# Pair's outputs stored from seven places, a third's operands made in pieces, next pair's raw loads bound to units

## The chip, the cores and the metric

The kernel runs on one core of a Trainium2 chip. The metric is the device time of one execution in microseconds (us); smaller is better. The engines are named as in the profile: PE (TensorE, matmuls), DVE (VectorE), ACT (ScalarE), POOL (GpSimd), SP (SyncE, which here only issues transfers).

## The reference, cut to what matters

Linear attention, then a gated feed-forward layer with an RMS norm, then a second feed-forward layer, in which the change lies:

```python
def _moe2_ref(x, w1, w2, w3, w_out) -> np.ndarray:
    h = np.maximum(np.maximum(x @ w1, x @ w2), x @ w3)
    return (h @ w_out).astype(np.float32)
# x 4608x512, w1, w2, w3 512x768, w_out 768x512, all float32
```

## The kernel before, in words

The 4608 tokens are nine groups of 512. Attention and the first layer run group by group and leave their results in device memory (`x2_dram`). The second layer then takes the first eight groups two at a time, which the code calls a **pair**, and the ninth alone. For a pair, `x @ w` is a two by two block product computed with seven block products instead of eight (A11, S2, S1, S3, A12, S4, A22 against the operands B11, T2, T1, T3, B21, B22, T4); three of the seven add onto a PSUM bank that already holds another.

Every float32 factor is split into a high and a low part, and each block product is six matmuls of 128x128 by 128x512 (`product2`, L488 to L494 in `three`). A **unit** is one weight matrix for one third of the 768 columns: seven block products, 42 matmuls, in four PSUM banks (G, V, a0, a1). A pair has nine units; three in a row (one for each of w1, w2, w3) make a **third**, and their maximum is kept in four SBUF tiles `t` (tags q, k, v, t; two buffers each). In a unit, PE fills the banks in the order A11 to G, S2 to V, S1 to a0, S3 to a1, then A12 onto G, S4 onto a0, A22 onto a1. Between them the other engines work: ACT copies G to `s1` (L749), DVE adds V to make `u2` (L751), ACT copies a0 to `s5` (L753), POOL adds the two to `w` (L754), and DVE adds `w` and a1 (L743 in the first unit of a third, else L745 followed by the maximum in L746). Only when that addition has read a1 may PE start A22, which adds onto a1.

When a third is done, `h_operands` makes its seven operands for the output product: four DVE subtractions (L797 to L810), and for each operand a high part cast by ACT (L91) and a low part subtracted by DVE (L92), eleven DVE and seven ACT instructions. For the first two thirds this code stands right behind the third's last unit. Behind the ninth unit, `out_pair` multiplies all three thirds with `w_out`, in eight banks, and gives eight output tiles of 128x512: two copied by ACT (L867), six added by DVE (L845). Each tile is written into one of three buffers (tag y) and stored to device memory from there.

Weights come from device memory in chunks of three block products (768 KB) through a ring of six tiles; a chunk is fetched into a ring place as soon as PE has read the old one (`consumed`). `load_raw` fetches the next pair's two groups (four tiles of 256 KB and two of 512 KB), and `combine` makes the four sums T1 to T4 from them with eight DVE subtractions (L603). A scheduler sorts instructions within what the data allow, and may pull code ahead of where it is written; each engine then runs its own list strictly in order, and SP issues all chunk fetches, raw loads and most stores from one list.

Of the kernel before, what the change touches and what calls it, by code (L numbers as in the profile page):

```python
# [15 lines left out]
P = 128  # L16
# [30 lines left out]
def attention_moe_moe(ctx: ExitStack, tc: tile.TileContext, q, k, kt, v, w1, rms_g, w2, w2_out, out):  # L47
# [486 lines left out]
                evacuate(acc[g][m], x2_dram[g][:, m, :], f"xe_{g}", m, 0.5)  # L534


    ring, fetched = {}, [0]
    wanted = [(p, c, None) for p in range(NPAIR) for c in range((UNITS + OUTS) * QUARTERS // CHUNK)]
    turns = [0, 1, 2, 3, UNITS, 4, 5, 6, 7, 8, UNITS + 1, UNITS + 2]
    single = [chunk_of(u, n) for u in turns for n in (A11, A12, S1, A22)]  # L540
# [2 lines left out]
    def fetch(count=1):  # L543
        for _ in range(count):
            i = fetched[0]
            if i >= len(wanted):
                return
            p, c, parts = wanted[i]
            t = wpool.tile([P, CHUNK, 2, N // 2], F32R, tag=RING[i % len(RING)], name=f"chunk_{p}_{c}")
            if parts is None:  # L550
                nc.sync.dma_start(t.bitcast(F32), chunk_dram[c])
            else:
                for n, (c, i) in enumerate(parts):
                    nc.sync.dma_start(t[:, n].bitcast(F32), chunk_dram[c][:, i])
            ring[p, wanted[fetched[0]][1]] = t
            fetched[0] += 1
# [170 lines left out]

    temps = []

    def unit(pr, u, t):  # L730

        fp, j = divmod(u, 3)
        a, b, c, d = (bank(tag, f"p2_{pr}_{u}_{tag}") for tag in ("G", "V", "a0", "a1"))
        if not temps:
            for tag in ("wh9", "wl9"):
                x = place(f"temps_{tag}", tag)
                temps.extend(x[:, i, :] for i in range(3))
        s1, s5, u2, w, y0, y1 = temps
        n = QUARTERS * u

        def largest(dst, x, pt, y):
            if j == 0:
                nc.vector.tensor_add(dst, x, pt)  # L743
            else:
                nc.vector.tensor_add(y, x, pt)  # L745
                nc.vector.tensor_max(dst, dst, y)  # L746

        product2(a, pr, n + A11, B11, True, True)
        nc.scalar.copy(s1, a)  # L749
        product2(b, pr, n + S2, T2, True, True)  # L750
        nc.vector.tensor_add(u2, s1, b)  # L751
        product2(c, pr, n + S1, T1, True, True)
        nc.scalar.copy(s5, c)  # L753
        nc.gpsimd.tensor_add(w, u2, s5)  # L754
        product2(d, pr, n + S3, T3, True, True)
        largest(t[1, 1], w, d, y0)
        product2(a, pr, n + A12, B21, False, True)
        if j == 0:
            nc.scalar.copy(t[0, 0], a)
        else:  # L760
            nc.vector.tensor_max(t[0, 0], t[0, 0], a)
        product2(c, pr, n + S4, B22, False, True)
        largest(t[0, 1], u2, c, y1)
        product2(d, pr, n + A22, T4, False, True)
        largest(t[1, 0], u2, d, y0)
# [58 lines left out]
        r = (2 * row + m) * P  # L824
        queue.dma_start(out[r : r + P, g * N : (g + 1) * N], e)

    def out_place(name):
        return two.tile([P, N], F32, tag="y", name=name, bufs=3)

    def out_pair(pr, t):  # L830
        g = 2 * pr
        a, b, c, d = ([bank(tag, f"o_{pr}_{tag}") for tag in tags] for tags in (
# [4 lines left out]
        for (pts, n, which), later in zip(steps, ((T1, T2), (T3, B21), (B22, T4), ())):  # L837
            out_product(pts, pr, n, which, (0, 1), True, False, False)
            for x in later:
                h_operands(2, t, x)  # L840
        u, w = temps[0:2], temps[2:4]

        def add(x, pt, row, col, m):
            e = out_place(f"oe_{pr}_{row}{col}_{m}")
            nc.vector.tensor_add(e, x, pt)  # L845
            store(e, row, g + col, m, nc.sync)

# [13 lines left out]
        for pts, n, which in ((a, A12, B21), (c, S4, B22), (d, A22, T4)):  # L861
            out_product(pts, pr, n, which, (0, 1, 2), False, True, True)
            consumed(pr, QUARTERS * UNITS + OUTS * (OUT_ORDER.index(n) + 1))
            for m in range(2):
                if n == A12:
                    e = out_place(f"oe_{pr}_00_{m}")
                    nc.scalar.copy(e, a[m])  # L867
                    store(e, 0, g, m, nc.scalar)
                elif n == S4:
                    add(u[m], c[m], 0, 1, m)  # L870
                else:
                    add(u[m], d[m], 1, 0, m)
# [7 lines left out]
            fetch()  # L880

    for pr in range(NPAIR):
        for u in range(UNITS):
            fp, j = divmod(u, 3)
            if j == 0:
                t = {
                    key: two.tile([P, N], F32, tag=tag, name=f"t2_{pr}_{fp}_{tag}")
                    for key, tag in (((0, 0), "q"), ((0, 1), "k"), ((1, 0), "v"), ((1, 1), "t"))
                }
            unit(pr, u, t)  # L890
            consumed(pr, QUARTERS * (u + 1))
            if pr == 0 and u == 0:
                out1(NG - 1, NF1 - 1)
                h_places()
            if j == 2 and fp < 2:
                for which in (B11, T1, T2, T3, B21, B22, T4):
                    h_operands(fp, t, which)
            if u == 1:
                load_raw(pr + 1)
            if 3 <= u < 7:  # L900
                for n in range(2 * u - 6, 2 * u - 4) if pr + 1 < NPAIR else range(2) if u == 3 else ():
                    combine(pr + 1, n)
        out_pair(pr, t)
        for which in range(7) if pr + 1 < NPAIR else (B11, B21, T1):
            split_operand(which)
# [114 lines left out]
```

## Time and profile before

| what | value |
|---|---|
| time, three runs | 1567.25 us median (1562.35, 1567.25, 1567.54) |
| time of the profiled execution | 1566.17 us |
| its span, first to last instruction | 1564.1 us |
| outside the span | 2.07 us |
| matmul busy time | 1519.6 us, 97% of the span |
| DVE, ACT, POOL busy time | 937.4, 568.7 and 217.8 us |
| mean granted TensorE clock | 0.992 of full speed |

The span is the program on the engines; the time adds what lies around it. A matmul's row in a trace is longer (0.39 us) than the step from one start to the next (0.23 us), because matmuls overlap; starts tell the pace. The second layer fills the span from about 1012 us to its end.

### The profile page before, as it was taken

Reading aid. Unit: us, or ns where it says so; the run is one execution under the profiler, and the core shown is the slowest. Engines: PE = TensorE matmul, PEld = TensorE weight load, DVE = VectorE, ACT = ScalarE, POOL = GpSimd, SP = SyncE. Lnnn points to the kernel's source line nnn. Section 1 sums busy time; section 2 is a strip of 40 time slices with the busy share of each in tenths; the row PEclk is TensorE's granted clock in tenths of the full one; section 3 lists DMA queues with packets and bytes.
Section 4 is the critical chain, followed back from the end, with each engine's and each line's share of the span. In section 5 each row is a group of like instructions: output and inputs, shape, how many; then the busy total and the mean of one; then the engine's idle time right before and its main releaser. Section 6 shows DMA issues by size and latency. Waiting matters only on the chain.

```text
span 1564.1 us, 18927 instructions
## 1 busy us (share of the span) xinstructions
PE 1519.6 (97%) x6902; PEld 1251.6 (80%) x6902; DVE 937.4 (60%) x1622; ACT 568.7 (36%) x1079; POOL 217.8 (14%) x279
## 2 busy tenths in 40 slices
PE   6899999999999999999999999999999999999999
PEld 4677888888888888888888888877877877877887
DVE  6999846655656666566553244556856846737622
ACT  6764533434334334334342232232422422413311
POOL 0000321221211221302212000011111101101100
PEclk8899999999999999999999999999999999999999
DMA  7842431432423324404313022155765665665473
GB/s 271 322 145 78 169 103 43 153 107 63 146 91 116 125 67 141 140 26 159 118 40 102 1 95 94 41 200 179 266 216 181 240 231 182 210 234 186 170 264 107
DMA packets 97837, 227.74 MB, mean 146 GB/s; under 512 B 9168, under 2 KB 33744, under 8 KB 97744
## 3 DMA queue, kind: packets, MB, share of 16 engines
q1 hardware_dynamic: 90832, 213.94, 40.9%
q10 hardware_dynamic: 6912, 12.59, 2.2%
q8 instruction: 55, 0.90, 0.2%
q14 instruction: 38, 0.31, 0.1%
HBM read 183.50 MB, written 42.99 MB: 145 GB/s over the span
## 4 chain that ended last, share of the span: by engine, by line
PE 82%; DVE 10%; DMA 3%; ACT 2%; POOL 1%; issue 1%; SPq 0%; DVEq 0%; ACTq 0%; POOLq 0%
PE pg L488 6%; PE pg L486 6%; PE pg L487 6%; PE pv L488 6%; PE pv L486 6%; PE acc L494 6%; PE acc L493 6%; PE pv L487 6%; PE acc L492 6%; PE p_a L492 3%; PE p_a L494 3%; PE p_a L493 3%; DMA out<-oe 2%; PE pk L326 2%; PE p_G L494 2%; PE p_G L493 2%
## 5 line engine op out<-in xcount | busy, mean ns | idle before, releaser
L658 DVE SCALAR_TENSOR_TENSOR t<-t,pg 128x512 f32<-128x512 f32 x106 | 72.7, 686 | 131.9 <-ACT t L657 130.3
L672 ACT CAST hh<-t 128x512 fp32r<-128x512 f32 x108 | 66.9, 620 | 154.0 <-DVE t L669 153.5
L676 DVE TENSOR_TENSOR hl<-t,hh 128x512 fp32r<-128x512 f32 x108 | 80.5, 745 | 54.5 <-ACT hh L672 53.8
L754 POOL TENSOR_TENSOR temps_wl<-temps_wh 128x512 f32<-128x512 f32 x36 | 48.8, 1355 | 457.0 <-ACT temps_wh L753 367.0
L492 PE MATMUL p_a<-x_wh,chunk 128*128 128x512 f32 x240 | 95.3, 397 | 16.1 <-DVE t_t L743 8.1
L657 ACT ACTIVATE t<-pg 128x512 f32<-128x512 f32 x106 | 62.9, 594 | 131.8 <-PE pg L488 131.8
L669 DVE TENSOR_TENSOR t<-t,pv 128x512 f32<-128x512 f32 x108 | 73.6, 682 | 60.6 <-PE pv L488 59.3
L231 POOL TENSOR_TENSOR wq<-st,wq 128x256 fp32r<-128x256 f32 x84 | 63.7, 773 | 221.0 <-ACT wq L230 218.0
L494 PE MATMUL p_a<-x_wh,chunk 128*128 128x512 f32 x240 | 93.9, 391 | 0.0
L493 PE MATMUL p_a<-x_wl,chunk 128*128 128x512 f32 x236 | 92.2, 391 | 0.0
L492 PEld LDWEIGHTS p_a<-x_wh,chunk 128*128 128x128 f32 x240 | 45.3, 189 | 30.6 <-DVE t_t L743 11.5
L749 ACT COPY temps_wh<-p_G 128x512 f32<-128x512 f32 x36 | 21.1, 587 | 118.0 <-PE p_G L494 95.6
L494 PEld LDWEIGHTS p_a<-x_wh,chunk 128*128 128x128 f32 x240 | 45.4, 189 | 9.6
L493 PEld LDWEIGHTS p_a<-x_wl,chunk 128*128 128x128 f32 x236 | 44.5, 188 | 9.2
L751 DVE TENSOR_TENSOR temps_wh<-temps_wh,p_V 128x512 f32<-128x512 f32 x36 | 24.6, 684 | 43.1 <-PE p_V L494 41.5
L290 POOL TENSOR_TENSOR q<-q,qm 128x512 f32<-128x512 f32 x28 | 30.8, 1099 | 125.5 <-DVE qm L281 103.6
L745 DVE TENSOR_TENSOR temps_wl<-temps_wl,p_a 128x512 f32<-128x512 f32 x24 | 16.4, 685 | 52.7 <-POOL temps_wl L754 52.7
L492 PE MATMUL p_G<-x_wh,chunk 128*128 128x512 f32 x123 | 47.9, 389 | 0.0
L494 PE MATMUL p_G<-x_wh,chunk 128*128 128x512 f32 x123 | 47.9, 389 | 0.0
L230 ACT CAST wq<-st 128x256 fp32r<-128x256 f32 x84 | 33.5, 420 | 32.4 <-DMA w_dram<-wq 23.9
L326 PE MATMUL pk<-v,k 128*128 128x129 f32 x300 | 39.8, 280 | 0.3 <-issue 0.3
L302 POOL TENSOR_TENSOR q<-q,qr 128x512 f32<-128x512 f32 x28 | 29.2, 1044 | 75.1 <-DVE qr L301 70.7
(681 smaller groups left out, 4468.9 us busy)
## 6 DMA issues: line engine op xcount, KB each, us to landing
chunk<-w_dram SPq DMA_DIRECT2D x112, 768.0 KB, 4.3
w_dram<-wq SPq DMA_DIRECT2D x84, 256.0 KB, 2.2
words<-in_w SPq DMA_DIRECT2D x24, 768.0 KB, 7.9
chunk<-w_dram SPq DMA_DIRECT2D x48, 256.0 KB, 3.7
k<-in_k SPq DMA_DIRECT2D x30, 320.0 KB, 3.6
v<-in_v SPq DMA_DIRECT2D x30, 320.0 KB, 4.1
st<-in_w SPq DMA_DIRECT2D x18, 512.0 KB, 4.6
x<-xe ACTq DMA_DIRECT2D x36, 256.0 KB, 2.5
```

Of the source, the lines that this page charges most:

```text
L231: nc.gpsimd.tensor_sub(t[:, 1, :], src, t[:, 0, :].bitcast(F32))
L326: nc.tensor.matmul(pk[:, 0 : P + 1], k_t[g, p][:, c, :], v_t[g, p][:, c, :], start=(c == 0), stop=(c == 4))
L486: nc.tensor.matmul(pt, hi[:, j, s], xhs[kk], start=(kk == 0), stop=False)
L487: nc.tensor.matmul(pt, hi[:, j, s], xls[kk], start=False, stop=False)
L488: nc.tensor.matmul(pt, lo[:, j, s], xhs[kk], start=False, stop=(kk == 3))
L492: nc.tensor.matmul(pt, ah, bh, start=first, stop=False, skip_group_check=onto)
L493: nc.tensor.matmul(pt, ah, bl, start=False, stop=False, skip_group_check=onto)
L494: nc.tensor.matmul(pt, al, bh, start=False, stop=last, skip_group_check=onto)
L658: nc.vector.scalar_tensor_tensor(t, t, 1.0, pg, op0=ALU.add, op1=ALU.mult)
L669: nc.vector.tensor_mul(t, t, pv)
L672: nc.scalar.copy(hh[g, f], t)
L676: nc.vector.tensor_sub(hl[g, f], t, hh[g, f].bitcast(F32))
```

## The change

Three things change, all in the second layer. **Stores.** `out_pair` writes its eight outputs into three tiles of tag y, the four tiles `t` of the last third (which nothing reads any more) and once more a tile of tag y, instead of only the three tiles of tag y. **Pieces.** The operands of a finished third are no longer written in one stretch: they are put into four groups (B11 and T1; T2; T3; B21, B22 and T4), and each group is bound behind one of the four DVE steps of the next unit (`u2`, then the three `largest`). `tc.issue_after` binds the scheduler's order and adds no wait by itself. **Raw loads and sums.** The next pair's raw loads are bound behind the chunk fetch last issued at unit 1, and its eight sums behind the DVE steps of units 4 and 5, four each.

```diff
@@ fetch
-                nc.sync.dma_start(t.bitcast(F32), chunk_dram[c])
+                fetches.append(nc.sync.dma_start(t.bitcast(F32), chunk_dram[c]).ins)
@@ unit
+        def then(ins):
+            with tc.issue_after(ins.ins):
+                for step, args in behind.pop(0) if behind else ():
+                    step(*args)
+
         def largest(dst, x, pt, y):
             if j == 0:
-                nc.vector.tensor_add(dst, x, pt)
+                then(nc.vector.tensor_add(dst, x, pt))
             else:
                 nc.vector.tensor_add(y, x, pt)
-                nc.vector.tensor_max(dst, dst, y)
+                then(nc.vector.tensor_max(dst, dst, y))
...
-        nc.vector.tensor_add(u2, s1, b)
+        then(nc.vector.tensor_add(u2, s1, b))
@@ out_pair
+        places = [two.tile([P, N], F32, tag="y", name=f"oe_{pr}_{i}", bufs=3) for i in range(3)]
+        places += [t[key] for key in ((0, 1), (1, 1), (1, 0), (0, 0))]
+        places.append(two.tile([P, N], F32, tag="y", name=f"oe_{pr}_3", bufs=3))
...
-            e = out_place(f"oe_{pr}_{row}{col}_{m}")
+            e = places.pop(0)
@@ the loop over pairs
-            unit(pr, u, t)
+            if 3 < u < 6 or u > 6:
+                todo = (range(0, 4) if u == 4 else range(4, 8) if u == 5 else ()) if pr + 1 < NPAIR else range(2) if u == 5 else ()
+                behind = [[(combine, (pr + 1, n))] for n in todo]
+            unit(pr, u, t, behind)
...
             if j == 2 and fp < 2:
-                for which in (B11, T1, T2, T3, B21, B22, T4):
-                    h_operands(fp, t, which)
+                behind = [
+                    [(h_operands, (fp, t, which)) for which in group]
+                    for group in ((B11, T1), (T2,), (T3,), (B21, B22, T4))
+                ]
             if u == 1:
-                load_raw(pr + 1)
-            if 3 <= u < 7:
-                for n in range(2 * u - 6, 2 * u - 4) if pr + 1 < NPAIR else range(2) if u == 3 else ():
-                    combine(pr + 1, n)
+                with tc.issue_after(fetches[-1]):
+                    load_raw(pr + 1)
```

The order of instructions shows what this moves. DVE, first pair, where its third unit ends and its fourth (`p_0_3`, the first of the second third) begins. Before, with the first third's operands made in one stretch (tiles `h_...`, and `t_0_0_...` for the differences):

```order
L797 TENSOR_TENSOR t_0_0_q<-t_0_0_k,t_0_0_q 128x512
L746 TENSOR_TENSOR t_0_0_v<-t_0_0_v,temps_wl_8550 128x512
L803 TENSOR_TENSOR t_0_0_k<-t_0_0_t,t_0_0_k 128x512
L92 TENSOR_TENSOR h_xl_8634<-t_0_0_q,h_xl_8633 128x512
L92 TENSOR_TENSOR h_ql<-t_0_0_v,h_qh 128x512
L800 TENSOR_TENSOR t_0_0_q<-t_0_0_t,t_0_0_q 128x512
L92 TENSOR_TENSOR h_xl_8636<-t_0_0_k,h_xl_8635 128x512
L751 TENSOR_TENSOR temps_wh_8549<-temps_wh_8549,p_0_3_V 128x512
L92 TENSOR_TENSOR h_xh_8632<-t_0_0_q,h_xh_8631 128x512
L743 TENSOR_TENSOR t_0_1_t<-temps_wl_8550,p_0_3_a_8810 128x512
```

The same place in the change:

```order
L757 TENSOR_TENSOR temps_wh_8549<-temps_wh_8549,p_0_3_V 128x512
L92 TENSOR_TENSOR h_xh_8630<-t_0_0_q,h_xh_8629 128x512
L803 TENSOR_TENSOR t_0_0_q<-t_0_0_k,t_0_0_q 128x512
L92 TENSOR_TENSOR h_xl_8634<-t_0_0_q,h_xl_8633 128x512
L749 TENSOR_TENSOR t_0_1_t<-temps_wl_8550,p_0_3_a_8792 128x512
L806 TENSOR_TENSOR t_0_0_q<-t_0_0_t,t_0_0_q 128x512
L92 TENSOR_TENSOR h_xh_8632<-t_0_0_q,h_xh_8631 128x512
L749 TENSOR_TENSOR t_0_1_k<-temps_wh_8549,p_0_3_a_8791 128x512
L809 TENSOR_TENSOR t_0_0_k<-t_0_0_t,t_0_0_k 128x512
L749 TENSOR_TENSOR t_0_1_v<-temps_wh_8549,p_0_3_a_8792 128x512
```

The unit's `u2` (L751, now L757) has moved ahead of all operand work, and three pieces now stand between it and the addition that reads a1 (L743, now L749). DVE in the next unit (`p_0_4`) of the change; before, nothing stood between these steps:

```order
L92 TENSOR_TENSOR h_kT<-t_0_0_t,h_sacc 128x512
L816 TENSOR_TENSOR t_0_0_q<-t_0_0_v,t_0_0_q 128x512
L757 TENSOR_TENSOR temps_wh_8549<-temps_wh_8549,p_0_4_V 128x512
L603 TENSOR_TENSOR sums_a<-raw_1_4_8718,raw_1_0_8710 128x512
L92 TENSOR_TENSOR x_wl_8538<-t_0_0_q,x_wl_8538 128x512
L751 TENSOR_TENSOR temps_wl_8550<-temps_wl_8550,p_0_4_a_8868 128x512
L752 TENSOR_TENSOR t_0_1_t<-t_0_1_t,temps_wl_8550 128x512
L603 TENSOR_TENSOR sums_a<-raw_1_4_8718,raw_1_1_8712 128x512
L767 TENSOR_TENSOR t_0_1_q<-t_0_1_q,p_0_4_G 128x512
```

Two of the next pair's sums (L603) and the last piece of T4 (`x_wl_8538`) have come in ahead of the maximum that reads G (L767). DVE at the end of the first pair, where `oe` and `o_` are `out_pair`'s tiles and banks and `p_1_0` is the next pair's first unit; before:

```order
L603 TENSOR_TENSOR sums_a<-raw_2_2_9554,sums_b 128x512
L603 TENSOR_TENSOR sums_b<-raw_2_3_9556,sums_b 128x512
L845 TENSOR_TENSOR oe_01_0_9367<-temps_wh_8549,o_acc_9205 128x512
L845 TENSOR_TENSOR oe_01_1_9370<-temps_wh_8549,o_a_9206 128x512
L845 TENSOR_TENSOR oe_10_0_9393<-temps_wh_8549,o_acc_9207 128x512
L751 TENSOR_TENSOR temps_wh_8549<-temps_wh_8549,p_1_0_V 128x512
L845 TENSOR_TENSOR oe_10_1_9396<-temps_wh_8549,o_a_9208 128x512
```

And in the change:

```order
L851 TENSOR_TENSOR oe_0_9275<-temps_wh_8549,o_acc_9207 128x512
L851 TENSOR_TENSOR oe_1_9276<-temps_wl_8550,o_a_9208 128x512
L851 TENSOR_TENSOR t_0_2_t<-temps_wh_8549,o_acc_9205 128x512
L851 TENSOR_TENSOR t_0_2_v<-temps_wh_8549,o_a_9206 128x512
L851 TENSOR_TENSOR t_0_2_q<-temps_wh_8549,o_acc_9207 128x512
L851 TENSOR_TENSOR oe_3_9278<-temps_wh_8549,o_a_9208 128x512
L757 TENSOR_TENSOR temps_wh_8549<-temps_wh_8549,p_1_0_V 128x512
```

The sums have left this place, and three of the last four outputs go to tiles `t_0_2_...` that no store occupies. SP's list keeps its stores where they were; the raw loads of pairs 2 and 3 and of the ninth group move from between chunks 24 and 27 of the pair before to one block behind chunk 9 of the pair in which they are written, and those of pair 1 from behind chunk 5 to behind chunk 9 of pair 0.

## Rows read from the trace of the kernel before

**Rows 1.** The page: busy time, share of the span, instructions.
```profile
PE 1519.6 (97%) x6902; PEld 1251.6 (80%) x6902; DVE 937.4 (60%) x1622; ACT 568.7 (36%) x1079; POOL 217.8 (14%) x279
```

**Rows 2.** Waits of PE: engine and line, waited for, us in total, times, longest.
```profile
PE p_a L492 <- DVE t_t L743: 8.1, 8, 1.0
PE p_a L492 <- DVE oe L845: 8.0, 5, 2.3
```

**Rows 3.** Timeline of PE, pair 0, fourth unit: start, duration, [idle before <-releaser].
```profile
1052.68 0.39 PE L494 MATMUL p_a<-x_wl,chunk 128*128 128x512 f32 x1
1054.08 0.50 PE L492 MATMUL p_a<-x_wh,chunk 128*128 128x512 f32 x1 [1.02 <-DVE t_t L743]
1054.42 0.39 PE L493 MATMUL p_a<-x_wh,chunk 128*128 128x512 f32 x1
```

**Rows 4.** Timeline of DVE and POOL in that unit.
```profile
1050.88 0.68 DVE L751 TENSOR_TENSOR temps_wh<-temps_wh,p_V 128x512 f32<-128x512 f32 x1
1051.47 0.68 DVE L92 TENSOR_TENSOR h_xh<-t_q,h_xh 128x512 fp32r<-128x512 f32 x1
1051.70 1.61 POOL L754 TENSOR_TENSOR temps_wl<-temps_wh 128x512 f32<-128x512 f32 x1 [10.19 <-DVE temps_wh L751]
1053.34 0.69 DVE L743 TENSOR_TENSOR t_t<-temps_wl,p_a 128x512 f32<-128x512 f32 x1 [1.18 <-POOL temps_wl L754]
```

**Rows 5.** Timeline, pair 0: third unit from its first matmul to the fourth unit's.
```profile
1035.23 0.39 PE L492 MATMUL p_G<-x_wh,chunk 128*128 128x512 f32 x1
...
1038.21 0.69 DVE L751 TENSOR_TENSOR temps_wh<-temps_wh,p_V 128x512 f32<-128x512 f32 x1 [1.38 <-PE p_V L494]
...
1039.56 0.59 ACT L753 COPY temps_wh<-p_a 128x512 f32<-128x512 f32 x1 [2.19 <-PE p_a L494]
...
1040.22 1.29 POOL L754 TENSOR_TENSOR temps_wl<-temps_wh 128x512 f32<-128x512 f32 x1 [8.23 <-ACT temps_wh L753]
...
1041.55 0.69 DVE L745 TENSOR_TENSOR temps_wl<-temps_wl,p_a 128x512 f32<-128x512 f32 x1 [2.64 <-POOL temps_wl L754]
1042.27 0.69 DVE L746 TENSOR_TENSOR t_t<-t_t,temps_wl 128x512 f32<-128x512 f32 x1
...
1042.99 0.63 ACT L91 CAST h_sacc<-t_t 128x512 fp32r<-128x512 f32 x1 [2.85 <-DVE t_t L746]
...
1044.75 0.39 PE L492 MATMUL p_G<-x_wh,chunk 128*128 128x512 f32 x1
```

**Rows 6.** Timeline of ACT, DVE and PE at the end of pair 0.
```profile
1123.08 0.59 ACT L867 COPY oe<-o_acc 128x512 f32<-128x512 f32 x1 [2.83 <-PE o_acc L494]
...
1131.39 0.59 ACT L867 COPY oe<-o_G 128x512 f32<-128x512 f32 x1 [7.72 <-DMA out<-oe]
...
1136.84 0.69 DVE L845 TENSOR_TENSOR oe<-temps_wh,o_acc 128x512 f32<-128x512 f32 x1 [9.45 <-DMA out<-oe]
...
1138.18 0.50 PE L492 MATMUL p_a<-x_wh,chunk 128*128 128x512 f32 x1 [2.20 <-DVE oe L845]
...
1140.80 0.50 PE L492 MATMUL p_a<-x_wh,chunk 128*128 128x512 f32 x1 [0.72 <-DVE oe L845]
```

**Rows 7.** Stretches: us, busy time of PE, PEld, DVE, ACT, POOL, PEclk, DMA share, GB/s.
```profile
1378.00:1380.00 2.00, 1.03 (x4) 0.86 (x5) 1.77 (x3) 0.38 (x1) 0.00 (x0) 1.00 0.10 39
1380.00:1384.00 4.00, 4.00 (x12) 3.12 (x11) 1.15 (x3) 0.79 (x2) 1.27 (x1) 0.57 0.94 266
```

**Rows 8.** Timeline of POOL and DVE in pair 0's ninth unit.
```profile
1099.98 1.35 POOL L754 TENSOR_TENSOR temps_wl<-temps_wh 128x512 f32<-128x512 f32 x1 [8.23 <-ACT temps_wh L753]
...
1100.10 1.79 DVE L92 TENSOR_TENSOR x_wl<-sums_a,x_wh 128x512 fp32r<-128x512 f32 x1
```

**Rows 9.** Transfers, 1012 to 1400 us, for chunk and raw: issue to landing.
```profile
DMA to landing us min/median/max: 4.0/4.3/10.1
...
DMA to landing us min/median/max: 2.9/3.8/5.4
```

**Rows 10.** Transfers out of the output tiles, 1012 to 1500 us.
```profile
DMA to landing us min/median/max: 2.0/5.6/7.9
```

More of the change, by code (lines that the diff above doesn't have):

```diff
@@ L534, in out1 @@
                 evacuate(acc[g][m], x2_dram[g][:, m, :], f"xe_{g}", m, 0.5)
-    ring, fetched = {}, [0]
+    ring, fetched, fetches = {}, [0], []
     wanted = [(p, c, None) for p in range(NPAIR) for c in range((UNITS + OUTS) * QUARTERS // CHUNK)]
@@ L728, in attention_moe_moe, with unit @@
     temps = []
-    def unit(pr, u, t):
+    def unit(pr, u, t, behind):
         fp, j = divmod(u, 3)
@@ L825, in store @@
         queue.dma_start(out[r : r + P, g * N : (g + 1) * N], e)
-    def out_place(name):
-        return two.tile([P, N], F32, tag="y", name=name, bufs=3)
     def out_pair(pr, t):
@@ L865, in out_pair @@
                 if n == A12:
-                    e = out_place(f"oe_{pr}_00_{m}")
+                    e = places.pop(0)
                     nc.scalar.copy(e, a[m])
@@ L882, in attention_moe_moe @@
     for pr in range(NPAIR):
+        behind = []
         for u in range(UNITS):
```

## Prediction

> **What bounds the kernel now.** I read the page first. PE is busy 97% of the span [rows 1], so only its waits can be won back. In the list of waits by pair of engines, two entries of PE lie in the second layer [rows 2]: eight waits for the DVE addition that reads bank a1 (t_t L743, 8.1 us) and five for the output additions (oe L845, 8.0 us). The other waits of PE lie in attention's start, far from the change.
>
> Next the timeline at one of each kind. After a wait of 1.02 us the start-to-start step is 1.40 us and the next 0.34 us [rows 3]. The normal step is a unit's 9.52 us over 42 matmuls, 0.227 us [rows 5]. So one such wait costs 1.17 + 0.11 = 1.28 us, 0.27 more than its idle time.
>
> Why PE waits there: in the fourth unit `u2` starts at 1050.88 and `w` runs on POOL at 1051.70, for 1.61 us, so that DVE adds `w` and a1 at 1053.34 [rows 4]. The unit began at 1044.75 [rows 5], so `u2` came 6.13 us into it; in the third unit it came at 1038.21 - 1035.23 = 2.98 us. DVE worked through the finished third's operands first. The eight waits are four pairs times two such thirds.
>
> At the end of pair 0, ACT's second output copy waits 7.72 us for a store of an earlier output and DVE's third addition 9.45 us [rows 6]. Only three places exist, and a store needs 2.0 to 7.9 us to land [rows 10]. Behind those additions PE waits 2.20 and 0.72 us, because the next unit wants banks a0 and a1. Three pairs' ends show it, the last pair's does not: five waits.
>
> At the third of these ends the granted clock was 1.00 over 1378 to 1380 us, in which PE was busy for only 1.03 of 2 us, and 0.57 over 1380 to 1384 us: the lower of its two levels, 1.2 GHz, for the greater part of those 4 us [rows 7]. A share x at half speed gives 1 - x/2 = 0.57, so x = 0.86, 3.4 us; half of it, 1.7 us, was lost.
>
> **What can be won.** Thirds: 8.1 + 8 x 0.27 = 10.3 us. Pair ends: 8.0 + 5 x 0.27 = 9.4 us. Clock: 1.7 us. Together 21.4 us.
>
> **The change part by part.** *Stores.* An output product per half is 9 matmuls, 9 x 0.227 = 2.04 us. The first half of A12 was ready when ACT copied it at 1123.08 [rows 6]; so the halves come ready near 1122.9, 1124.9, 1126.9, 1129.0, 1131.0 and 1133.0 us. The second to fifth go to the four `t` tiles, which nothing occupies. The last takes the first output's place again. That place was free by 1131.4, when ACT wrote its second copy there [rows 6], before 1133.0 us, and the first addition now comes sooner. Even 4 us more would be hidden, since the next unit wants a1 only after three more products, 3 x 1.36 = 4.08 us (a product is 6 matmuls, 1.36 us). The next unit's `s1` and `u2` follow on time. DVE also loses eight sums from this place, which frees it earlier. I take the full 9.4 us and the clock's 1.7 us.
>
> On the fall of the clock the Trainium skill has a rule: the page "TensorE: Matmul & The Clock Gate", section "What's actually happening", says that the low clock is the default, that activity lifts it, and that the window over which the chip judges this runs free of the kernel. The trace agrees in that of three similar pauses one was followed by a fall. By that rule any of the three ends may pay 1.7 us in a given run, so this term would be 0 to 5.1 us; by the rows it is 1.7 us.
>
> *Pieces, in the first unit of the next third.* All times from that unit's start. DVE's back-to-back step is 0.60 us (1050.88 to 1051.47) [rows 4]. `u2` at 2.98; B11's low part 3.6; T1's difference 4.2 to 4.9. ACT's `s5` starts at 4.33 and ends at 4.92 as in the third unit [rows 5]; its cast of T1 (about 0.6 us) ends at 5.6. POOL's `w` runs 4.99 to 6.28 [rows 5]. Here a contention enters: a DVE subtraction of two SBUF tiles that started 0.12 us after such a `w` took 1.79 us instead of 0.68, until 0.56 us after `w` had ended [rows 8]. So T1's low part, which would start at 5.6, ends near 6.9; then a1's addition, 6.9 to 7.6. PE wants it at 6 x 1.36 = 8.16. No wait, with 0.56 us to spare. Between both ends: all eight waits gone, or, if the pieces hold the addition as long as now, none. I take gone.
>
> *The next unit.* T2 to T4 fill DVE: T2's difference 7.5, its low part 8.9 (ACT's copy of G, ready at 5 x 1.36 = 6.8, comes before the cast), a0's addition 9.5, T3's difference 10.1, a1's second addition 10.7, three low parts 11.3 to 13.1, T4's difference 13.1 to 13.8. `u2` then comes at 13.7 instead of 9.52 + 2.98 = 12.5, one sum at 14.3, T4's low part 14.9 to 15.6. ACT casts T4 at 13.8 to 14.4, so `s5` slips from 13.85 to 14.4 to 15.0. `w` meets T4's low part, waits for it and runs 15.6 to 16.8. a1's addition 16.85 to 17.55, due at 9.52 + 8.16 = 17.68. The maximum in t follows 0.72 us after it (1041.55 to 1042.27) [rows 5], 17.6; the second sum 18.2; the maximum that reads G 18.8 to 19.5. PE wants G at 2 x 9.52 = 19.04. A new wait of about 0.45 us, 0.72 us with its restart, in the three pairs that have sums there: 2.2 us. Bounds: 0 without the contention, and 3 x 1.3 = 3.9 us at the length of today's waits. I take 2.2, as the worked one. Behind the second third nothing of sums stands there, so the maximum comes 0.6 us earlier, inside its time.
>
> Units 4 and 5 carry 13 and 12 DVE steps, 7.8 us at most of 9.52; unit 3 has 15, 9.0 us. Total DVE work is unchanged.
>
> *Raw loads.* They stand behind chunk 9, whose ring place is free when PE has read chunk 3, 12 products, 16.3 us into the pair. The first sum wants them at 4 x 9.52 + 3.6 = 41.7 us. Six loads land 2.9 to 5.4 us after issue [rows 9], so even one after another (6 x 5.4 = 32) the last would be only 7 us late, and they overlap. Chunk 10 queues behind them: place free at 15 products, 20.4 us, wanted at 30 products, 40.8 us, against landings of 10.1 us at the slowest. Cost nothing; hidden under units 1 to 3.
>
> The skill's page "DMA: Bandwidth & Descriptors", section "Rules for kernel authors", says to issue a transfer early and wait for it late. This part does the reverse of its first half; by that rule the sums would stall. The trace's 25 us between issue and use speak against a stall here.
>
> **Sum.** 21.4 - 2.2 = 19.2 us gained. The profiled execution took 1566.17 us, so 1547.0; on the median, 1567.25, it would be 1548.0. I say 1547.
>
> **Rivals.** *A, the pieces only move the wait.* DVE runs its list in order, so anything late in the three pieces (ACT's cast of T1, which stands behind `s5`) holds a1's addition, as now. For it: only 0.56 us to spare. Against: ACT has no other work there. It decides if T1's low part ends past 7.5 us. Then the thirds keep 10.3 us: 1566.2 - 21.4 + 10.3 + 2.2 = 1557.
>
> *B, the pair ends stay.* If the last place is not free, or stores queue behind the four chunk fetches of that time, DVE waits as before in front of the next `u2`. It decides when the first output's place is free 5 us later than 1131.4. Keeping 11.1 us: 1566.2 - 10.3 + 2.2 = 1558.
>
> *C, slower: raw loads.* If a raw tile lands later than 25 us after its issue, DVE's list stops at the first sum, and PE a few products later. Each us of it counts three times. To end 0.5% above, 1575, it needs 19.2 + 7.8 = 27 us, 9 us a pair, so loads that land 25 + 9 = 34 us after issue; the slowest raw load took 5.4 [rows 9].
>
> *D, the order does not hold.* If the scheduler undid the binding, nothing changes: 1566. The printed order shows it holds.
>
> **How the numbers follow.** Forecast 0.75, A 0.11, B 0.06, C 0.03, D and unnamed others that eat most of the gain 0.05. Range: low end 1566.2 - 21.4 = 1544.8, less 4 us for a run that falls low (1562.35 lies 4.9 under the median): 1541. High end: without A and B 1547 + 1.7 (the largest new waits) + 1.1 (median), 1550; with part of A, 1556. A measurement of this kernel tells 0.5%, 7.8 us, from no change: faster ends at 1559.4. Forecast, A and nearly all of B are faster, 0.90; same 0.07; slower 0.03.
>
> **What would show it.** Right: no wait of PE for t_t in the first unit of a third, `u2` there 3 us into the unit; no DVE wait on a store longer than 1 us at pair ends, no PE wait for oe; a small wait of PE for the maximum in t_q at unit 5's start, under 1 us, three times; granted clock 1.00 throughout pair ends. Wrong: waits of PE above 1 us at A22 (A), of DVE on out<-oe (B), or of DVE on raw (C).

## The result and the profile after

| | before | the change |
|---|---|---|
| median | 1566.26 us (4 runs, 1562.35 to 1567.54) | 1546.45 us (4 runs, 1545.93 to 1546.94) |
| ratio, 95% interval | | 0.9878 [0.9859, 0.9896] |
| profiled execution | 1566.17 us | 1545.93 us |
| its span | 1564.1 us | 1544.2 us |

The kernel is 19.8 us faster by the medians and 20.2 us by the two profiled executions; the forecast was 1547.0 us. The page's busy line of the change, against [rows 1]:

```profile
PE 1515.2 (98%) x6902; PEld 1250.9 (81%) x6902; DVE 939.6 (61%) x1622; ACT 567.4 (37%) x1079; POOL 215.8 (14%) x279
```

Every engine has as many instructions as before, and their busy times differ by under 5 us. So the gain is for the most part idle time of PE, whose busy time fell by 4.4 us. The list of waits of PE, asked for the second layer alone (1012 to 1500 us), answers [rows 2] with its heading and no entry:

```profile
engine line waited for: us in total, times, longest us
```

Times of whole executions hide part of this, since attention and the first layer end 1 to 2 us earlier or later from one execution to the next. So I also measure the second layer alone, from the start of its first matmul (into `p_G`) to the start of its last (into `o`). These are the two rows of the change:

```profile
1013.98 0.39 PE L492 MATMUL p_G<-x_wh,chunk 128*128 128x512 f32 x1
...
1540.05 0.39 PE L494 MATMUL o<-h_wh,chunk 128*128 128x512 f32 x1
```

That is 526.07 us, against 546.54 us before (1013.47 to 1560.01): 20.47 us less, all of the gain.

**A third's boundary.** DVE and POOL in pair 0's fourth unit, against [rows 4]. The unit began at 1045.26 us:

```profile
1048.25 0.69 DVE L757 TENSOR_TENSOR temps_wh<-temps_wh,p_V 128x512 f32<-128x512 f32 x1 [1.38 <-PE p_V L494]
...
1049.57 0.69 DVE L803 TENSOR_TENSOR t_q<-t_k,t_q 128x512 f32<-128x512 f32 x1
...
1050.95 1.15 DVE L92 TENSOR_TENSOR h_xl<-t_q,h_xl 128x512 fp32r<-128x512 f32 x1 [0.69 <-ACT h_xl L91]
1052.03 0.68 DVE L749 TENSOR_TENSOR t_t<-temps_wl,p_a 128x512 f32<-128x512 f32 x1
```

`u2` comes 2.99 us into the unit instead of 6.13, and the addition that reads a1 runs from 6.77 to 7.45 us. PE wants the bank at 8.16 us, so it does not wait.

**The unit after it.** DVE, PE and (last two rows, one `w` of each of the two units) POOL, at the end of pair 0's fifth unit:

```profile
1060.00 0.68 DVE L92 TENSOR_TENSOR x_wl<-t_q,x_wl 128x512 fp32r<-128x512 f32 x1
1061.87 0.69 DVE L751 TENSOR_TENSOR temps_wl<-temps_wl,p_a 128x512 f32<-128x512 f32 x1 [1.18 <-POOL temps_wl L760]
...
1063.19 0.69 DVE L603 TENSOR_TENSOR sums_a<-raw,raw 128x512 f32<-128x512 f32 x1
1063.80 0.68 DVE L767 TENSOR_TENSOR t_q<-t_q,p_G 128x512 f32<-128x512 f32 x1
...
1064.07 0.39 PE L494 MATMUL p_a<-x_wh,chunk 128*128 128x512 f32 x1
1064.53 0.50 PE L492 MATMUL p_G<-x_wh,chunk 128*128 128x512 f32 x1
1064.87 0.40 PE L493 MATMUL p_G<-x_wh,chunk 128*128 128x512 f32 x1
...
1050.26 1.29 POOL L760 TENSOR_TENSOR temps_wl<-temps_wh 128x512 f32<-128x512 f32 x1 [8.23 <-DVE t_q L803]
1060.10 1.73 POOL L760 TENSOR_TENSOR temps_wl<-temps_wh 128x512 f32<-128x512 f32 x1 [8.55 <-DVE sums_a L603]
```

Here is what is left. The maximum that reads G ends at 1064.48 us, and PE's first matmul into G starts 0.46 us after the one before it, the next one 0.34 us after that. Over two plain steps of 0.227 us that is 0.34 us lost, though the idle time in it is only 0.07 us. It happens in three pairs (1064.53, 1179.20 and 1293.87 us): 1.0 us in all.

**A pair's end.** ACT and DVE at the end of pair 0, against [rows 6]:

```profile
1123.39 0.59 ACT L873 COPY t_k<-o_G 128x512 f32<-128x512 f32 x1 [1.47 <-PE o_G L494]
...
1125.44 0.69 DVE L851 TENSOR_TENSOR t_t<-temps_wh,o_acc 128x512 f32<-128x512 f32 x1 [4.26 <-PE o_acc L494]
...
1131.62 0.69 DVE L851 TENSOR_TENSOR oe<-temps_wh,o_a 128x512 f32<-128x512 f32 x1 [1.41 <-PE o_a L494]
1134.36 0.69 DVE L757 TENSOR_TENSOR temps_wh<-temps_wh,p_V 128x512 f32<-128x512 f32 x1 [2.05 <-PE p_V L494]
```

These outputs now wait for PE, where before they waited 7.7 and 9.5 us for a store (the last row is the next unit's `u2`). The clock does not fall: around the third pair's end (the next pair's first matmul starts at 1360.68 us) PE is busy throughout and PEclk is 1.00, where [rows 7] had 0.57:

```profile
1355.00:1378.00 23.00, 23.00 (x103) 19.05 (x102) 7.39 (x12) 2.94 (x5) 2.58 (x2) 1.00 0.83 298
```

**Transfers.** Issue to landing of the raw loads (1012 to 1400 us, against the last row of [rows 9]), and of all eight stores of a pair (1012 to 1500 us, against [rows 10]):

```profile
DMA to landing us min/median/max: 5.5/6.3/8.7
...
DMA to landing us min/median/max: 4.2/6.8/8.4
```

Both got slower: six loads are now issued together, and more stores are under way at once. No engine that computes waits for either in the second layer.

### The profile page after: what moved, and what is told of

Same layout as the page of the kernel before. It is cut to its first block, busy times and chain, and to the rows that moved or that the text cites. A ratio compares the mean times of both kernels' runs of the same rounds, so it can differ in the third digit from the quotient of the medians.

```text
span 1544.2 us, 18937 instructions
## 1 busy us (share of the span) xinstructions
PE 1515.2 (98%) x6902; PEld 1250.9 (81%) x6902; DVE 939.6 (61%) x1622; ACT 567.4 (37%) x1079; POOL 215.8 (14%) x279
## 4 chain that ended last, share of the span: by engine, by line
PE 91%; DVE 6%; issue 1%; ACT 1%; DMA 0%; POOL 0%; SPq 0%; DVEq 0%; ACTq 0%
PE pg L486 6%; PE pg L488 6%; PE pg L487 6%; PE pv L486 6%; PE acc L492 6%; PE pv L488 6%; PE acc L493 6%; PE acc L494 6%; PE pv L487 6%; PE p_a L493 4%; PE p_a L494 4%; PE p_a L492 4%; PE p_G L492 2%; PE p_G L493 2%; PE p_G L494 2%; PE pk L326 2%
## 5 line engine op out<-in xcount | busy, mean ns | idle before, releaser
L757 DVE TENSOR_TENSOR temps_wh<-temps_wh,p_V 128x512 f32<-128x512 f32 x36 | 24.6, 684 | 33.8 <-PE p_V L494 33.8
L751 DVE TENSOR_TENSOR temps_wl<-temps_wl,p_a 128x512 f32<-128x512 f32 x24 | 16.4, 685 | 37.1 <-POOL temps_wl L760 37.1
```

## The experiments

My theory, as forecast: each of the first two parts removes its own waits (places 11.1 us with the clock, pieces 10.3 us), the third part is worth nothing in itself, and its sums bring the new wait. The rivals are that a part only moves its waits, and that the third part is what frees the pair ends. All results in one table. "Before" is the kernel before on the same chip; the second layer's length is that of the profiled execution.

| kernel | median us | before us | ratio, 95% interval | second layer us |
|---|---|---|---|---|
| before | 1566.26 | | | 546.54 |
| the change | 1546.45 | 1566.26 | 0.9878 [0.9859, 0.9896] | 526.07 |
| e1 places alone | 1555.89 | 1564.18 | 0.9944 [0.9932, 0.9955] | 535.46 |
| e2 pieces alone | 1553.68 | 1564.18 | 0.9930 [0.9918, 0.9942] | 534.69 |
| e3 raw loads and sums alone | 1560.16 | 1564.18 | 0.9977 [0.9967, 0.9986] | 539.72 |
| e4 change without places | 1553.11 | 1563.33 | 0.9934 [0.9922, 0.9946] | 534.32 |
| e5 change without pieces | 1554.51 | 1563.33 | 0.9944 [0.9932, 0.9957] | 535.05 |
| e6 change without raw and sums | 1545.27 | 1563.33 | 0.9885 [0.9871, 0.9898] | 524.93 |
| e7 a later sum | 1545.30 | 1564.18 | 0.9878 [0.9865, 0.9891] | 524.93 |
| e8 four places | 1544.98 | 1563.33 | 0.9884 [0.9869, 0.9900] | 526.05 |
| e9 raw loads two units later | 1547.06 | 1563.66 | 0.9894 [0.9880, 0.9909] | 525.78 |
| e10 first sum behind `w` | 1544.80 | 1563.66 | 0.9880 [0.9865, 0.9894] | 524.98 |
| e11 the change again | 1545.72 | 1563.66 | 0.9886 [0.9870, 0.9903] | 526.10 |
| e12 two parts, four places | 1544.80 | 1563.66 | 0.9880 [0.9865, 0.9895] | 524.94 |

### e1: the places alone

```diff
+        places = [two.tile([P, N], F32, tag="y", name=f"oe_{pr}_{i}", bufs=3) for i in range(3)]
+        places += [t[key] for key in ((0, 1), (1, 1), (1, 0), (0, 0))]
+        places.append(two.tile([P, N], F32, tag="y", name=f"oe_{pr}_3", bufs=3))
...
-            e = out_place(f"oe_{pr}_{row}{col}_{m}")
+            e = places.pop(0)
...
```

> The kernel before with the seven store places alone (outputs of a pair's end go to three y tiles, then to the four tiles of the finished third, then to a y tile); pieces, raw loads and sums as before. My theory: each part of the change removes its own waits and they add up. The places alone take away the matrix engine's waits on an output's addition at the pair ends (9.4 us in four pairs, the first of them 8.0) and the clock fall at the third pair's end (1.7 us), so 11.1 us: about 1555 us; the eight waits of 1.28 us at the boundaries of thirds stay. Rival: the pair-end additions are late because of what the vector engine does just before them (the last sums and the low parts of the third), not for want of a place; then the waits stay and the time is 1565 to 1566 us.

All of PE's waits in the second layer of e1:

```profile
PE p_a L492 <- DVE t_t L743: 8.1, 8, 1.0
```

The output's waits are gone and the clock did not fall; the boundary waits stand as in [rows 2]. The second layer is 11.08 us shorter, the forecast's 11.1. By the times it is 8.3 us (7.0 to 10.6): the kernel before ran 2 us faster on this chip than in its profiled execution, from which the 11.1 was read. The rival falls: for want of places the additions were late, with the sums still standing there.

### e2: the pieces alone

```diff
...
-                for which in (B11, T1, T2, T3, B21, B22, T4):
-                    h_operands(fp, t, which)
+                behind = [
+                    [(h_operands, (fp, t, which)) for which in group]
+                    for group in ((B11, T1), (T2,), (T3,), (B21, B22, T4))
+                ]
```

> The kernel before with the pieces alone: a finished third's operands are made behind readings of the next unit; places, raw loads and sums as before. My theory: the eight waits of 1.28 us at the thirds' boundaries go (10.3 us), the new wait at unit 5's start does not come up, since the sums are not behind unit 4's readings, and the pair ends stay as they are: about 1556 us. Rival: the sums, which are not bound to anything here, land between the pieces and make one of the readings late in each pair, so that about half comes back: 1560 us or more.

All of PE's waits in the second layer of e2, and one stretch at the third pair's end (columns as in [rows 7]):

```profile
PE p_a L492 <- DVE oe L851: 6.7, 5, 2.1
```

```profile
1370.00:1373.00 3.00, 3.00 (x9) 2.34 (x9) 0.96 (x2) 0.96 (x2) 0.20 (x1) 0.59 0.95 238
```

The boundary waits are gone and no new one has come; the pair-end waits are there, 1.3 us less of them, and so is the fall of the clock, again at the third pair's end. The second layer is 11.85 us shorter: 10.3 us as forecast, and some 1.6 us of shorter pair-end waits, which no step of mine had foreseen. Most of it is at the second pair's end: PE waited 1.19 us instead of 2.31, and the first three stores landed 6.2 to 6.5 us after their issue instead of 7.1 to 7.4. Why they landed sooner is not shown.

### e3: raw loads and sums alone

```diff
-                load_raw(pr + 1)
-            if 3 <= u < 7:
-                ...
-                    combine(pr + 1, n)
+                with tc.issue_after(fetches[-1]):
+                    load_raw(pr + 1)
...
+                behind = [[(combine, (pr + 1, n))] for n in todo]
```

> The kernel before with the third part alone: next pair's raw loads issued behind unit 1's last chunk, and the sums bound behind readings of units 4 and 5; places and operands as before. My theory: nothing waits for raw loads or sums, so this alone is worth nothing; 1565 to 1568 us, with the eight boundary waits and the pair-end waits still there (perhaps one more wait of 0.3 us in three pairs at unit 5's start, 1 us). Rival: loads that no longer share the queues with the output stores, and sums that no longer stand near a pair's end, are what freed the pair ends; then 3 to 10 us go, 1556 to 1563 us.

My expectation was wrong here: 4.0 us by the times (2.2 to 5.2), 6.8 us in the second layer of the profiled execution. PE's waits there:

```profile
PE p_a L492 <- DVE t_t L749: 7.7, 8, 1.4
PE p_a L492 <- DVE oe L851: 3.7, 3, 1.5
```

Three output waits of 3.7 us instead of five of 8.0, and no fall of the clock. Why, the timeline of DVE at the end of pair 0 shows. Before:

```profile
1121.97 1.82 DVE L603 TENSOR_TENSOR sums_b<-raw,sums_a 128x512 f32<-128x512 f32 x2 [0.49 <-DMA raw<-x]
1123.71 0.68 DVE L845 TENSOR_TENSOR oe<-temps_wh,o_acc 128x512 f32<-128x512 f32 x1
...
1139.46 0.69 DVE L751 TENSOR_TENSOR temps_wh<-temps_wh,p_V 128x512 f32<-128x512 f32 x1 [0.73 <-ACT temps_wh L749]
1140.06 0.68 DVE L845 TENSOR_TENSOR oe<-temps_wh,o_a 128x512 f32<-128x512 f32 x1
```

And in e3:

```profile
1122.11 0.69 DVE L851 TENSOR_TENSOR oe<-temps_wh,o_acc 128x512 f32<-128x512 f32 x1 [1.65 <-POOL temps_wh L864]
...
1139.06 0.68 DVE L851 TENSOR_TENSOR oe<-temps_wh,o_a 128x512 f32<-128x512 f32 x1
1139.87 0.69 DVE L757 TENSOR_TENSOR temps_wh<-temps_wh,p_V 128x512 f32<-128x512 f32 x1
```

Before, sums stood in front of the first output (and one waited for a raw load), and the last output stood behind the next unit's `u2`, where it made the second wait of each end. In e3 the first output is written 3.0 us sooner, counted from the second layer's start (1122.11 - 1014.87 against 1123.71 - 1013.47), the last one stands ahead of `u2`, and the second wait is gone. So the rival is right for this part by itself: the sums' place was part of why the pair ends were late. The part moves the raw loads too, and no run takes the two apart; but the stores landed no sooner than before (median 5.6 us in both), which speaks against the loads' place in the queues. Moving the sums does not cure it, and e1 shows that the places do so with the sums still there.

### e4, e5 and e6: the change without one of its parts

e4 takes the places back, e5 the pieces, e6 the bound raw loads and sums: the edits of e1, e2 and e3 with their signs turned, made in the changed kernel. For e4:

```diff
...
-            e = places.pop(0)
+            e = out_place(f"oe_{pr}_{row}{col}_{m}")
...
```

> The changed kernel with the three y tiles only for the eight outputs (pieces, bound raw loads and bound sums stay). With the third part alone the first wait at each of three pair ends was still there, but 1.63, 1.54 and 0.98 us over a plain step instead of 2.2 to 2.5, and the second one was gone. My theory now: the places are what takes away the rest, so here those three waits of 1.0 to 1.6 us with 0.11 us each come back and nothing else: 4.5 us, about 1551 us, no boundary waits, and the matrix engine waits for oe three times. Rival: with the operands in pieces the last third's end also finishes earlier and the stores have all the time they need; then the places are not needed any more, 1546 to 1547 us.

All of PE's waits in the second layer of e4, and a stretch at the second pair's end:

```profile
PE p_a L492 <- DVE oe L851: 5.7, 3, 2.0
```

```profile
1255.00:1258.00 3.00, 3.00 (x9) 2.33 (x8) 0.49 (x2) 0.58 (x1) 1.28 (x1) 0.50 0.95 236
```

Three output waits came back, but of 1.8 to 2.0 us rather than 1.0 to 1.6, and with them a fall of the clock. So the second layer is 8.25 us longer than the change's, not the 4.5 I expected; the change's three small waits at unit 5's start, too short for this list, are there as well. Why the pauses are longer than in e3 can be read at pair 0's end: in both, the last outputs stand behind two stores in a row, and the second took 6.5 us to land here against 5.8 in e3. Why it did is not shown. The places are needed.

> The changed kernel with the operands of a finished third in one stretch again (places, bound raw loads and bound sums stay). My theory: eight waits of about 1.2 us over a plain step, with 0.11 us each, come back in front of the product that adds onto bank a1, four of them one unit away from where they stood, since what the scheduler puts first has changed: 10 us, about 1556.5 us; no waits for oe. Rival: the stretch also makes the last third's end late, and some of the pair-end waits come back with it: 1558 us or more.

All of PE's waits in the second layer of e5:

```profile
PE p_a L492 <- DVE t_t L749: 7.7, 8, 1.4
```

Eight waits and nothing at pair ends. The second layer is 8.98 us longer than the change's: the eight waits cost 9.9 us, and the new wait of 1.0 us is not there.

> The changed kernel with next pair's raw loads and sums where the scheduler had put them before (places and pieces stay). Theory 1: with seven places the additions at a pair's end do not wait for stores, so the sums that stand there cost nothing, and the third part of the change is worth nothing or less than nothing: no waits at all in the second layer, since no sum stands in front of the maximum at unit 5; 1545 to 1546 us. Theory 2: the gain that the third part showed by itself, 4.0 us, comes on top: sums that wait for raw loads at a pair's end hold the additions, and the matrix engine waits again: 1549 to 1550 us.

Theory 1: there is no wait of PE in the second layer at all (no step from one matmul's start to the next is over 0.30 us, and so it is in e7, e10 and e12), which is 524.93 us long, 1.14 us shorter than the change's. The sums do stand at the pair ends again and one waits 1.6 us for a raw load, as DVE's waits show, but the outputs behind them have places and are in time:

```profile
DVE sums_a L603 <- DMA raw<-x: 1.6, 1, 1.6
```

So the third part is worth 6.8 us alone and -1.1 us beside the two others. The three parts' gains in the second layer add to 11.1 + 11.9 + 6.8 = 29.8 us, and together they give 20.5: places and third part work on the same waits.

### e7 and e10: the new wait

e7 moves the second sum behind unit 4's readings one place on, out of the way of the maximum that reads G. e10 moves the first one as well, from behind `u2` to behind the addition of `w` and a1. What counts of the edit is one line; e7's, then e10's:

```diff
-                todo = (range(0, 4) if u == 4 else ...
+                todo = (((0,), (), (1, 2), (3,)) if u == 4 else ...
```

```diff
+                todo = (((), (0,), (1, 2), (3,)) if u == 4 else ...
```

> The changed kernel with one thing moved: of the four sums behind unit 4's readings one is taken from behind the maximum of its second half and put two readings on, so that the maximum that frees bank G is no longer behind a sum. My theory: the only waits that are new in the changed kernel, 0.34 us at unit 5's start in three pairs (the first product waits for the maximum that reads its bank), go, and nothing else moves: 1.0 us less, about 1545.5 us. Rival: the sum that was moved makes the next maximum late, and as much is lost at unit 5's later products: no difference, 1546.5 us. If the two cannot be told apart by the time, the matrix engine's start-to-start steps at unit 5's start do (0.34 us over a plain step of 0.227 us, or none).

No wait is left in the second layer; it takes 524.93 us, 1.14 us less than in the change. The rival's late maximum does not show.

> The changed kernel with the first of the four sums of unit 4 moved from behind u2 to behind the addition of w and a1, and the second one reading on, where there is one sum in front of the maximum that reads bank G, as in the changed kernel. What is tested is the contention of the vector engine and GpSimd: in the changed kernel the low part of T4 starts 0.10 us before GpSimd's addition w, which takes 1.73 us instead of 1.29. Without the sum the low part starts 0.6 us sooner, if its cast is done. My theory: w takes about 1.3 us, the addition of w and a1 and all behind it come 0.4 us sooner, and the waits of 0.34 us at unit 5's start are gone though the number of steps in front of the maximum is reduced by none behind w: 1.0 us less than the changed kernel, 1545.4 us. Rival: the sum itself, not the contention, is what makes the maximum late; then w still takes 1.7 us and the wait stays, 1546.4 us.

DVE and POOL in e10's fifth unit, `u2` at 1059.33 us:

```profile
1060.10 0.69 DVE L92 TENSOR_TENSOR x_wl<-t_q,x_wl 128x512 fp32r<-128x512 f32 x1
1061.97 0.69 DVE L751 TENSOR_TENSOR temps_wl<-temps_wl,p_a 128x512 f32<-128x512 f32 x1 [1.18 <-POOL temps_wl L760]
...
1060.63 1.31 POOL L760 TENSOR_TENSOR temps_wl<-temps_wh 128x512 f32<-128x512 f32 x1 [8.55 <-ACT temps_wh L759]
```

`w` starts 1.30 us behind `u2`, as in the change, but takes 1.31 us instead of 1.73: T4's low part overlaps it by 0.16 us instead of 0.58. So the addition of `w` and a1 comes 2.64 us behind `u2` instead of 3.07. DVE idles 1.18 us in front of that addition in both kernels, so what was saved there is the stretch of `w` and not the sum's own step. One sum still stands between that addition and the maximum, as in the change, and the wait is gone. So either cure does: one sum less behind that addition (e7, where `w` still takes 1.73 us), or less contention in front of it. On the chip that ran e10 and the change (e11) side by side, e10 took 1543.93 to 1545.38 us and the change 1545.60 to 1546.08: about 0.9 us by the medians.

### e11: the change on the same chip

The kernel is the change itself, with no edit.

> The changed kernel once more, on the chip of the other three kernels of this call, so that they can be compared with it: 1545 to 1547 us, three waits of 0.34 us at unit 5's start and no others in the second layer.

It held: 1545.72 us, and the same three waits and no others.

### e8 and e12: how many places, how many parts

```diff
-        places = [two.tile([P, N], F32, tag="y", name=f"oe_{pr}_{i}", bufs=3) for i in range(3)]
-        places += [t[key] for key in ((0, 1), (1, 1), (1, 0), (0, 0))]
-        places.append(two.tile([P, N], F32, tag="y", name=f"oe_{pr}_3", bufs=3))
+        places = []
+        for i in range(2):
+            places += [two.tile([P, N], F32, tag="y", name=f"oe_{pr}_{3 * i + k}", bufs=3) for k in range(3)] + [t[0, 1]]
```

> The changed kernel with four store places instead of seven: three y tiles and one tile of the finished third, used twice in turn. The halves of the outputs come 2.04 us apart and a store landed 4.4 to 8.4 us after its issue, median 7.4. My theory: the fifth output can be written 4 x 2.04 = 8.2 us after the first, about when the first store lands, and what is late by 1 or 2 us is hidden, since the next pair's first unit wants its banks only 4.1 us after the last output: the time of the changed kernel, 1546.5 us, with waits of the vector engine or of the scalar engine on stores of 0 to 2 us, and none of the matrix engine. Rival: the waits pass on from output to output, so that the last addition comes over 4 us late and the matrix engine waits as before: 1549 us or more.

DVE at the end of pair 0 in e8:

```profile
1126.79 0.69 DVE L851 TENSOR_TENSOR oe<-temps_wh,o_acc 128x512 f32<-128x512 f32 x1 [6.83 <-DMA out<-oe]
...
1130.40 0.69 DVE L851 TENSOR_TENSOR t_k<-temps_wh,o_a 128x512 f32<-128x512 f32 x1 [1.41 <-PE o_a L494]
```

The fifth output waits for a store, 2.6 us longer than it would wait for PE (6.83 us against the 4.26 us of the change's row at 1125.44). Two outputs later DVE is back on PE's pace. PE's second layer is that of the change, 526.05 us. Four places are enough. (The median of 7.4 us that I had expected with is that of the change's four stores out of `oe` tiles in a pair; over all eight it is 6.8.)

e12 is e8 with raw loads and sums put back as they were before.

```diff
             if u == 1:
-                with tc.issue_after(fetches[-1]):
-                    load_raw(pr + 1)
+                load_raw(pr + 1)
+            if 3 <= u < 7:
+                ...
+                    combine(pr + 1, n)
```

> The smallest version that should give everything: operands in pieces and four store places, with raw loads and sums where the scheduler had put them before. My theory: each of the two parts removes its own waits and the third part is not needed: no wait of the matrix engine in the second layer, 1545 us. Rival: with sums at the pair's end the first stores go out 1.6 us later, so four places are too few there and one or more waits for an output come back: 1547 us or more.

The outputs do wait for stores at the pair ends, seven times, but PE has no wait in the second layer, 524.94 us:

```profile
DVE oe L851 <- DMA out<-oe: 21.1, 7, 6.8
```

21 us of idle DVE time cost nothing here. 1544.80 us is, with e10, the lowest median of all; e6, e7, e8, e10 and e12 lie too close to be told apart by times.

### e9: raw loads two units later

```diff
-            if u == 1:
+            if u == 3:
                 with tc.issue_after(fetches[-1]):
                     load_raw(pr + 1)
```

> The changed kernel with next pair's raw loads bound behind the chunk fetched last at unit 3 instead of unit 1: behind chunk 14, whose ring place is free when chunk 8 has been read, 27 products of 1.36 us, 36.7 us into the pair, instead of 16.9. In the changed kernel the last of the six landed 11.2 us after the first was issued. My theory (the mechanism of the slower rival): they land up to 48 us into the pair, the first sum wants its tiles at 42, so the vector engine waits 4 to 6 us for raw tiles in front of an addition that the matrix engine wants at 46.2, and in three pairs the matrix engine waits 1 to 4 us each: 1550 to 1558 us, best guess 1553. Rival: the first tiles land early enough and the sums wait only for the last, behind the urgent addition: under 1548 us.

In pair 0 the loads were issued from 1054.66 us on, 21 us later than in the change. DVE's only sizeable wait for them there:

```profile
1064.76 1.29 DVE L603 TENSOR_TENSOR sums_a<-raw,raw 128x512 f32<-128x512 f32 x2 [0.61 <-DMA raw<-x]
```

The scheduler put the first two sums behind the maximum that reads G, where in the change the first one ran at 1059.40 us, so the urgent addition was not held. The change's three waits at unit 5's start are gone; two smaller ones are new, for the same maximum at unit 6's start (0.25 us idle at 1074.94, and 0.2 us lost at 1303.75), and the second layer is 0.3 us shorter than the change's. The median is 1.3 us above e11's all the same. In the profiled executions that difference is not in the second layer: e9's began 0.9 us later than e11's (1014.66 against 1013.77 us). I did not find its cause. The rival stands: two units later is still no loss that PE shows.

## Why the prediction was right, and where its steps were not

**Thirds, 10.3 us: right.** The steps held to 0.1 or 0.2 us: T1's low part was forecast from 5.6 to near 6.9 us into the unit and ran from 5.69 to 6.84; the addition on a1 6.9 to 7.6, measured 6.77 to 7.45. The spare time was 0.7 us, so rival A, which needed the low part past 7.5 us, was 0.7 us away. e2 and e5 give the term from both sides.

**Pair ends, 9.4 us, and the clock, 1.7 us: right in size.** e1 shows 11.1 us for the places. The last place was free in time: the first output's store landed at 1128.27 us, and those of the other two `y` tiles by 1129.60, 2.0 us before the eighth output. That rules out rival B, and e8 shows that even a fifth output 2.6 us late is hidden by the three products that I had counted.

**The clock's rule.** I had weighed the rule of the Trainium skill's page "TensorE: Matmul & The Clock Gate", section "What's actually happening", against one fall in three pauses. Three kernels with pauses of 1.2 to 2.3 us now show it: before (2.20, 2.31 and 2.07 us, a fall after the last), e2 (1.99, 1.19, 2.08, a fall after the last) and e4 (2.04, 1.80, 1.85, a fall after the second, the shortest). That agrees with a clock judged without regard to where the kernel stands; which pause is hit cannot be read from its length. One execution of each kernel was profiled, so it is not shown that the fall moves from one execution of the same kernel to the next.

**The new wait, 2.2 us: right in place, too large.** It measured 1.0 us, and this is the term of the sum that was mis-sized. The step that failed was "`w` meets T4's low part, waits for it and runs 15.6 to 16.8": it started at 14.84 us, 0.10 us after the low part (all counted from the fourth unit's start), took 1.73 instead of 1.29 us and ended at 16.57. The maximum ended at 19.2 instead of 19.5 us, and the idle time was 0.07 instead of 0.45 us. The restart cost is as forecast, 0.27 us over the idle time. Putting 1.0 for 2.2 makes the sum 1545.8 us, against 1545.93 for the profiled execution.

**Raw loads at no cost: right, with a wrong row under it.** They took 5.5 to 8.7 us to land, not the 2.9 to 5.4 us of [rows 9], which came from loads issued one by one. The 25 us between issue and use made that harmless. Rival C had no case: in e9 the loads went out 21 us later and PE's second layer did not grow. I had read the rule of the Trainium skill's page "DMA: Bandwidth & Descriptors", section "Rules for kernel authors", as a threat of a stall, and the part as its reverse. The rule (issue early, wait late) speaks of no stall, and against their use the loads now go out earlier than before, not later: before, the last load of pair 0 was issued at 1116.98 us and read at 1121.97, and in the change at least 23 us lie between. No run shows a gain from that.

**"DVE also loses eight sums from this place, which frees it earlier": priced at nothing, and right only beside the places.** By itself, e3, it is worth 6.8 us of second layer; with places, e6, less than nothing. The total came out right because I had credited the pair ends once.

## What to carry to other kernels

Parts that work on the same wait don't add: three gains that sum to 29.8 us gave 20.5 us together, and one of the three was better left out. When PE is the bound, price each part by the one wait that it removes, then ask what is next late in that stage; the length of the stage in the trace, from its first to its last matmul, tells 1 us where whole times of one kernel vary by 1 to 5. Before new work is put into a gap of an engine's list, count the slots up to the reading that the bound engine needs next: a sum one reading later (e7) cost nothing, one reading sooner 1.0 us.

## What the runs showed of the hardware

**DVE and GpSimd take turns, and either can be the one that waits.** A DVE subtraction of two SBUF tiles that started 0.69 us after `w` on POOL took 1.15 us instead of 0.68 (1050.95), until 0.55 us after `w` had ended; one that started 0.10 us before `w` took its 0.68 us, and `w` took 1.73 instead of 1.29 (1060.10). I had taken `w` for an operation that starts late, not one that stretches. On the Trainium skill's page "SBUF — State Buffer", the section "Who interferes with whom" says that a DVE instruction with two SBUF inputs and a GpSimd instruction that reads SBUF exclude each other, and that issue order decides which one blocks. These rows agree, in both orders, and e10 shows it by taking most of the overlap away.

**An idle time that hardly shows costs more than it is long.** 0.07 us of idle PE time cost 0.34 us: the step into the late matmul took 0.46 us and the one after it 0.34 us, where both are 0.227 us otherwise. A list of waits that leaves out such small entries is empty while 1.0 us is still there; only start-to-start steps show it.

**Transfers that are issued together land later.** Six raw loads in one block took a median of 6.3 us against 3.8, and a pair's stores 6.8 us against 5.6. The other kernels agree: 5.9 to 6.2 us in the eight more that issue the block, e9 at another place among them, and 3.7 to 4.0 in the four more that do not; stores 6.1 to 7.1 us with four or seven places, 5.2 to 5.7 with three. Counting from rows of another place in the program was wrong by more than half for the loads.
